# A new order of key tiles in the first attention layer, lent buffers and a second mixer buffer, in a two-layer attention and mixer kernel

## The chip, the cores and the metric

One core of one Trainium2 chip. The metric is the device time of one execution in microseconds (us); medians of several executions are given. Every ratio is to runs of the kernel before on the same chip in the same rounds.

Engines: PE is TensorE, ACT is ScalarE, DVE is VectorE, POOL is GpSimd, SP is the engine whose queue issues most transfers. A "block" below is one 128 x 512 square of attention scores (one head, one tile of 128 keys, 512 queries).

## The reference, cut to what matters

Batch 1, 2048 rows, width 448, 16 heads of 28, bf16 in and out. The same weights serve both layers.

```python
def _A_ref(x, wqkv, wo):                       # attention
    q, k, v = split(x @ wqkv)                  # 16 heads of 28
    p = softmax(q k^T * 28 ** -0.5)            # 2048 x 2048 for each head
    return (p v) @ wo
def _B_ref(x, w1, w2, w3, w4):                 # mixer and MLP
    h = gelu(layernorm(x) @ w1)
    hs = concat(h shifted by -1, +1, -2, +2 rows, a quarter of the columns each) @ w2
    x1 = x + hs
    return x1 + gelu(layernorm(x1) @ w3) @ w4
for layer in range(2):
    x = x + _A_ref(layernorm(x), ...)
    x = x + _B_ref(layernorm(x), ...)
```

## The kernel before

A small scheduler in Python lays out the instructions of all engines before the program is built. Each job (projection of K, evacuation, mixer of a group of tiles, ...) is a generator that yields operations with an assumed duration; the scheduler places them by readiness and priority. The program then gives each engine its list in that order.

The queries are cut into chunks, the keys into tiles of 128. A *segment* is one chunk, one group of four heads and a run of key tiles. `ORDER` lists (chunk, first tile, end tile) in the order in which ScalarE meets them, four head groups each; layer 0 is "layer one":

```python
CHUNKS = {0: [(0, 4), (4, 4), (8, 4), (12, 2), (14, 2)], ...}          # first row tile, row tiles
ORDER = {0: [(0, 0, 4), (0, 4, 8), (0, 8, 16), (1, 0, 16), (2, 0, 16), (3, 0, 16), (4, 0, 16)],
         1: [(0, 0, 7), (1, 0, 7), (0, 7, 11), (1, 7, 11), (0, 11, 16), (1, 11, 16), (2, 0, 16), ...]}
RANK = {...}      # priorities: ('k', layer, c) K and V of a key chunk, ('q', layer, chunk),
                  # ('a', ...) output projection and first half of the mixer, ('b', ...) second half
D_RATE = {...}    # share of blocks whose exponential VectorE takes
```

A segment waits for its Q and for the K of its tiles. A chunk that comes back to later keys needs a correction (`fct`), a shift of its Q, and its partial sum in DRAM:

```python
def seg_ready(si, kts):
    yield ("wait", ("q", L, CHUNKS[L][ch][0] // 4, g))
    if not first:
        yield ("wait", ("qp", si))
    for c in sorted(set(kc_of(L, k) for k in kts)):
        yield ("wait", ("k", L, g, c))
```

ScalarE evaluates blocks in turns of three and two PSUM banks, while VectorE takes a few blocks with an integer trick and a polynomial, five instructions each:

```python
yield op("act", 0.06 + n * w * 0.000833, lambda e, ...: e.activation(out=PT[:, s0:s0 + n, 0:w],
         in_=ps[:, bk[0]:bk[0] + n, 0:w], func=ACT.Exp, scale=SCALE), ...)
```

The mixer's hidden rows of a group of up to four tiles go into one buffer, `h2T`; pairs of tiles of the second layer use idle V slots instead:

```python
side = not direct and L == 1 and n == 2
hname = "h2V" if side else "h2T"
```

PE is kept busy with matmuls on the identity where it has nothing else (`filler`). The scheduler places one when PE's counted load in a short window is under `TARGET`.

## Time and profile before

| | before |
|---|---|
| median | 1077.07 us (1076.42 to 1079.06, 3 runs) |
| profiled span | 1074.8 us |
| ScalarE busy | 1020.3 us (95%) |
| blocks on VectorE | 37 of 2048 |
| ScalarE idle from 17 to 100 us | 9.6 us |
| after the last exponential | 47.5 us |

How to read the profile: a row of a group gives the line, the engine, what it writes and reads, the count, busy time and mean duration, then the idle time of its engine just before it and who ended it. In the views of stretches the engines come in the order PE, PEld (weight loads), DVE, ACT, POOL, then the granted TensorE clock, the DMA share and GB/s. In a timeline the bracket gives the idle time before the first instruction of the row. The lines themselves stand in the prediction.

### The profile page before, as it was taken

The numbers are of one execution on the slowest core, as the hardware profiler recorded it, in microseconds if no ns is written. First come the engines' busy times: TensorE is split into PE (matmuls) and PEld (weight loads), VectorE is DVE, ScalarE is ACT, GpSimd is POOL, SyncE is SP. The second block draws the span as 40 slices with busy tenths as digits, with TensorE's granted clock in tenths as the row PEclk, the third lists the DMA queues.
The fourth block names the chain that finished last, engine by engine and source line by source line (L and its number), as shares of the span: only waits on it lengthen the run. The fifth ranks groups of instructions, "written<-read, shape, count | busy, mean of one in ns | idle before, by whom it ended". The sixth has DMA issues, their size and how long they took to land.

```text
span 1074.8 us, 35355 instructions
## 1 busy us (share of the span) xinstructions
PE 1010.3 (94%) x16037; PEld 422.5 (39%) x16037; DVE 619.8 (58%) x1236; ACT 1020.3 (95%) x920; POOL 312.9 (29%) x506
## 2 busy tenths in 40 slices
PE   7999999999999999999999998999999999999998
PEld 2333443443333433343433433353333433444455
DVE  7776569836468236765156553514797484444442
ACT  6898999999999999999999999999999999999952
POOL 2244125201254024452032201102743130432111
PEclk9999999999999999999999999999999999999999
DMA  4547221103111022120221123313411110220000
GB/s 115 138 110 208 83 57 32 24 17 91 32 32 32 13 78 56 44 42 22 63 58 40 41 85 95 133 50 110 89 27 21 43 39 16 59 49 16 12 11 32
DMA packets 95494, 62.26 MB, mean 58 GB/s; under 512 B 68528, under 2 KB 85248, under 8 KB 95344
## 3 DMA queue, kind: packets, MB, share of 16 engines
q1 hardware_dynamic: 91968, 51.92, 18.7%
q0 software_dynamic: 3376, 8.09, 2.7%
q8 instruction: 125, 2.05, 0.8%
q14 instruction: 25, 0.20, 0.1%
HBM read 27.12 MB, written 15.71 MB: 40 GB/s over the span
## 4 chain that ended last, share of the span: by engine, by line
ACT 72%; PE 18%; DVE 8%; issue 1%; DMA 0%; SPq 0%; DVEq 0%
ACT PT L1455 65%; PE ps L770 11%; ACT h2T L1852 4%; PE ps L1300 4%; PE ps L761 3%; ACT fb L1703 1%; ACT L1852 1%; DVE fb L1364 1%; DVE fb L1362 1%; ACT L1455 1%; DVE hT L1704 1%; DVE fb L1702 1%; DVE yd L1341 1%; DVE PD L1369 1%; DVE xn L962 0%
## 5 line engine op out<-in xcount | busy, mean ns | idle before, releaser
L1455 ACT ACTIVATE PT<-ps 128x1536 bf16<-128x1536 f32 (+1 forms) x805 | 920.8, 1339 | 14.2 <-PE ps L1300 13.2
L1300 PE MATMUL ps<-qT,kT 32*128 32x512 bf16 (+1 forms) x2560 | 315.0, 340 | 28.5 <-ACT PT L1455 19.8
L761 PE MATMUL ps<-PT,vaug 128*32 128x512 bf16 (+1 forms) x2523 | 250.3, 340 | 0.0
L1300 PEld LDWEIGHTS ps<-qT,kT 32*128 32x128 bf16 x2560 | 80.7, 91 | 300.6 <-ACT PT L1455 272.2
L1893 PE MATMUL ps<-ident 128*32 128x256 bf16 x3804 | 166.6, 274 | 3.4 <-POOL ident L850 1.5
L770 PE MATMUL ps<-xT,w 128*32 128x512 bf16 (+2 forms) x1600 | 126.5, 360 | 2.5 <-DVE h2T L1837 1.6
L1893 PEld LDWEIGHTS ps<-ident 128*32 128x32 bf16 x3804 | 107.8, 96 | 31.2 <-issue 12.3
L770 PE MATMUL ps<-w,h2T 128*32 128x448 bf16 x1512 | 106.3, 365 | 13.8 <-ACT h2T L1852 12.9
L1837 DVE CAST h2T<-ps 128x512 bf16<-128x512 f32 (+2 forms) x112 | 67.8, 606 | 79.5 <-PE ps L770 69.8
L761 PEld LDWEIGHTS ps<-PT,vaug 128*32 128x32 bf16 x2523 | 74.8, 95 | 93.4 <-issue 80.4
L1560 POOL TENSOR_TENSOR otn<-ub,fb 128x512 bf16<-128x512 f32 (+1 forms) x36 | 40.2, 1116 | 179.9 <-DMA fb<-rscr 179.7
L1096 POOL TENSOR_TENSOR sq<-kT 128x512 bf16<-128x512 bf16 (+2 forms) x32 | 29.9, 935 | 120.2 <-DVE kT L1110 120.0
L770 PEld LDWEIGHTS ps<-w,h2T 128*32 128x32 bf16 x1512 | 41.1, 98 | 51.7 <-issue 18.4
L1701 POOL TENSOR_TENSOR fb<-hT 112x512 f32<-112x512 bf16 (+1 forms) x36 | 37.5, 1044 | 79.2 <-DVE hT L1684 75.7
L770 PEld LDWEIGHTS ps<-xT,w 128*32 128x32 bf16 x1600 | 43.7, 95 | 42.6 <-issue 18.1
L1341 DVE TENSOR_SCALAR yd<-ps 128x512 int32<-128x512 f32 x37 | 25.1, 682 | 39.5 <-PE ps L1300 39.1
L1787 POOL TENSOR_TENSOR x_res<-x_res,x1b 128x448 f32<-128x448 f32 x32 | 38.9, 1222 | 20.9 <-DVE xn L967 20.8
L1534 DVE COPY ub<-ps 128x512 f32<-128x512 f32 (+1 forms) x40 | 23.3, 582 | 35.1 <-PE ps L761 34.8
L953 POOL TENSOR_SCALAR vpe<-mv 128x1 f32<-128x1 f32 (+2 forms) x21 | 5.5, 261 | 129.2 <-DVE mv L948 129.2
L1852 ACT ACTIVATE h2T<-h2T 128x7168 bf16<-128x7168 bf16 (+2 forms) x8 | 42.0, 5244 | 0.1
L1536 DVE SCALAR_TENSOR_TENSOR ub<-ub,fct,ps 128x512 f32<-128x512 f32 x24 | 17.9, 746 | 41.0 <-PE ps L761 40.7
L770 PE MATMUL ps<-kT,w 128*32 128x512 bf16 (+2 forms) x576 | 40.4, 360 | 1.1 <-DMA kT<-xn 1.0
(168 smaller groups left out, 1208.0 us busy)
## 6 DMA issues: line engine op xcount, KB each, us to landing
uscr<-ub SPq DMA_DIRECT2D x24, 256.0 KB
ub<-uscr SPq DMA_DIRECT2D x24, 256.0 KB
fb<-rscr SPq DMA_DIRECT2D x24, 256.0 KB
xnd<-xn SPq DMA_DIRECT2D x28, 128.0 KB, 2.2
x_res<-in_A_x_dram POOLq DMA_DIRECT2D x16, 224.0 KB, 4.0
xd<-x_res SPq DMA_DIRECT2D x16, 224.0 KB, 2.7
x_res<-xd SPq DMA_DIRECT2D x16, 224.0 KB, 3.0
out_dram<-obf SPq DMA_DIRECT2D x16, 112.0 KB
```

The source lines that it names most:

```text
L761: return lambda e: e.matmul(out=out, lhsT=lhsT, rhs=rhs, start=start, stop=stop, **kw)
L770: r.append(e.matmul(out=out[c:c + w, :], lhsT=lhsT[:, c:c + w], rhs=rhs, start=start, stop=stop, tile_position=(0, c)))
L1096: return op("pool", 0.15 + NW * 0.0018, lambda e: e.tensor_tensor(out=sq[:, si, 0:NW], in0=src, in1=src, op=ALU.mult), reads=rk, writes=[( ...
L1300: yield op("pe", max(0.055, 0.22 / nc_ * NW / 512.0), lambda e, i=i, kc=kc, j=j, g=g, a=a, NW=NW, bank=bank: e.matmul(out=ps[:, bank, i * ...
L1341: yield op("dve", c_ps(512), lambda e: e.tensor_scalar(out=y, in0=ps[:, bi(bank), :], scalar1=SCALE * L2E * FS, scalar2=-126.0 * FS, op0=A ...
L1455: yield op("act", 0.06 + n * w * 0.000833, lambda e, bk=bk, s0=s0, n=n, w=w: e.activation(out=PT[:, s0:s0 + n, 0:w], in_=ps[:, bk[0]:bk[0] ...
L1560: yield op("pool", 0.2 + NW * 0.0021, lambda e: e.tensor_tensor(out=otn[:, g, 0:NW], in0=u, in1=rb[:, 0:NW], op=ALU.mult), reads=[uk, fk], ...
L1701: yield op("pool", 0.2 + NW * 0.00165, lambda e: e.tensor_tensor(out=f, in0=z, in1=z, op=ALU.mult), reads=hk, writes=[fk])
L1787: yield op("pool", 1.2, lambda e: e.tensor_tensor(out=X, in0=X, in1=X1, op=ALU.add), reads=[xk, ("x1b", s)], writes=[xk], deps=[nop_])
L1837: ev = op("dve", c_ps(NW), lambda e, fch=fch, b=b: e.tensor_copy(out=hb[:, fch, 0:NW], in_=ps[:, bi(b), 0:NW]), reads=[("ps", bi(b))], wri ...
L1852: yield op("act", c_act(nl * NW), lambda e: e.activation(out=hb[:, 0:nl, 0:NW], in_=hb[:, 0:nl, 0:NW], func=ACT.Gelu_apprx_tanh), reads=al ...
L1893: return [e.matmul(out=ps[32 * c:32 * c + 32, bi(b), 0:256].rearrange("p (a n) -> p a n", n=128), lhsT=ident[:, 32 * c:32 * c + 32], rhs=i ...
```

## The change

The intent: while K and V of tiles 4 to 15 are still being made, let ScalarE work on the first four key tiles for *two* query chunks, so that the later keys are due later. With it: more buffers for VectorE's exponentials in V slots that are idle for a while, look-ahead of these exponentials over the end of a segment, a second mixer buffer for groups of up to four tiles, and all priorities, rates and margins drawn anew. The loads of w3 and w4 at segment 9 are the same in both kernels. The core of the diff (cut):

```diff
-ORDER = {0: [(0, 0, 4), (0, 4, 8), (0, 8, 16), (1, 0, 16), (2, 0, 16), ...
+ORDER = {0: [(0, 0, 4), (1, 0, 4), (0, 4, 8), (0, 8, 16), (1, 4, 16), (2, 0, 16), ...
-DPRIO = 5
+DPRIO = 1.5
-DSEG = 0
+DSEG = 1
-XSHUT = (10, 50)
+XSHUT = (16, 61)
-RANK = {... [('b', 0, 0), ('a', 0, 0), ('k', 0, 1), ('b', 0, 1), ('k', 0, 2), ('k', 1, 0), ('q', 0, 2), ('q', 0, 1), ...
+RANK = {... [('q', 0, 1), ('b', 0, 1), ('b', 0, 0), ('a', 0, 0), ('k', 1, 0), ('q', 0, 3), ('k', 0, 1), ...
-D_RATE = {(0, 0): 0.08, (0, 1): 0.05, (0, 2): 0.05, (0, 3): 0.06, (1, 0): 0.16, (1, 1): 0.1, (1, 2): 0.16}
+D_RATE = {(0, 0): 0.08, (0, 1): 0.045, (0, 2): 0.05, (0, 3): 0, (1, 0): 0.015, (1, 1): 0.1, (1, 2): 0.03}
-Sched.TARGET = 0.64
+Sched.TARGET = 0.6
-FTH = 0.03
+FTH = 0.15
...                                   # other margins of the scheduler
+        def xtra(kind):
+            for ph, base in ((0, 16), (1, 9)):
+                if ("xopen", ph) in SC.events and ("xshut", ph) not in SC.events:
+                    return {"y": ["yv%d" % base, "yv%d" % (base + 2)], "f": ["fv%d" % (base + 4)], "pd": ["pv%d" % (base + 6)]}[kind]
+            return []
...
-                        got = yield ("try", [MISC[0:2], YS, PDS])
+                        got = yield ("try", [MISC[0:2], xtra("y") + YS, xtra("pd") + PDS])
...
-            side = not direct and L == 1 and n == 2
-            hname = "h2V" if side else "h2T"
...
+                hname = yield ("acq", ["h2T", "h2W"] if ("xdone", 1) in SC.events else ["h2T"], [("xT", xt)])
+                wide = hname == "h2W"
```

A branch that would give blocks to POOL is in the new code as well, but its rates are all 0. Factors and shifts get a pair index (`PI`), because two chunks now come back from different points.

## The prediction

> **What bounds the kernel now.** I read the page first (busy shares, slices, chain), then the waits of ScalarE, then the stretches of the span, then ScalarE's timeline at the start. The page:
>
> ```profile
> span 1074.8 us, 35355 instructions
> PE 1010.3 (94%) x16037; PEld 422.5 (39%) x16037; DVE 619.8 (58%) x1236; ACT 1020.3 (95%) x920; POOL 312.9 (29%) x506
> PE   7999999999999999999999998999999999999998
> ACT  6898999999999999999999999999999999999952
> ACT 72%; PE 18%; DVE 8%; issue 1%; DMA 0%; SPq 0%; DVEq 0%
> ```
>
> ScalarE (ACT) is busy for 1020.3 of 1074.8 us and makes 72% of the chain that ended last. PE shows 94%, but 166.6 us of that are matmuls on the identity that only keep it busy (L1893), so PE has room in most stretches; ACT has none. ACT's work by shape:
>
> ```profile
> L1455 ACT ACTIVATE PT<-ps 128x1536 bf16<-128x1536 f32 x402 | 623.4, 1551 | 6.1 <-PE ps L1300 5.2
> L1455 ACT ACTIVATE PT<-ps 128x1024 bf16<-128x1024 f32 x402 | 453.5, 1128 | 8.1 <-PE ps L1300 8.0
> L1852 ACT ACTIVATE h2T<-h2T 128x7168 bf16<-128x7168 bf16 x4 | 24.7, 6178 | 0.0
> ```
>
> The exponentials come in pairs of three and two blocks of 512. 402 x 3 + 402 x 2 + 1 = 2011 blocks; the problem has 2 layers x 16 heads x 16 key tiles x 4 query chunks = 2048, so 37 blocks go to VectorE (its group for yd has x37, 25 of them between 100 and 340 us, 12 after 500 us). Everything is a question of when ACT is idle. The stretches, engine busy times in the order PE, PEld, DVE, ACT, POOL:
>
> ```profile
> 0.00:17.00 17.00, 10.31 (x111) 4.50 (x111) 11.82 (x50) 10.13 (x14) 6.27 (x19) 1.00 0.65 180
> 17.00:51.00 34.00, 30.23 (x430) 10.84 (x425) 26.89 (x63) 31.56 (x31) 6.43 (x9) 1.00 0.42 103
> 51.00:88.00 37.00, 35.45 (x486) 11.90 (x486) 27.24 (x63) 29.84 (x28) 16.19 (x20) 1.00 0.51 143
> 88.00:180.00 92.00, 87.56 (x1392) 36.19 (x1391) 63.79 (x119) 92.00 (x83) 31.12 (x45) 1.00 0.32 85
> 180.00:520.00 340.00, 320.32 (x5340) 135.12 (x5341) 200.04 (x363) 338.24 (x296) 107.85 (x170) 0.99 0.16 39
> 520.00:780.00 260.00, 250.29 (x3613) 98.34 (x3605) 127.57 (x273) 258.33 (x229) 64.75 (x103) 0.99 0.28 78
> 780.00:1026.00 246.00, 230.23 (x3823) 98.32 (x3820) 144.54 (x274) 243.72 (x211) 70.56 (x120) 1.00 0.14 31
> 1026.00:1074.80 48.80, 45.89 (x860) 27.26 (x860) 17.86 (x38) 16.48 (x34) 9.72 (x21) 1.00 0.07 24
> ```
>
> Length less ACT busy gives its idle time: 6.9 us before the first exponential, 2.4 + 7.2 us from 17 to 88 us, 0.0 + 1.8 + 1.7 + 2.3 us in the 938 us after that, and 32.3 us in the tail after the last exponential. So there are only two places to gain idle time: the first 88 us and the tail. The timeline of ACT between 44 and 96 us shows what the first one is:
>
> ```profile
> 43.55 7.04 ACT L1455 ACTIVATE PT<-ps 128x1024 bf16<-128x1024 f32 x6
> 54.54 11.41 ACT L1455 ACTIVATE PT<-ps 128x1024 bf16<-128x1024 f32 x10 [3.96 <-PE ps L1300]
> 65.92 18.47 ACT L1455 ACTIVATE PT<-ps 128x1024 bf16<-128x1024 f32 x16
> 87.98 7.80 ACT L1455 ACTIVATE PT<-ps 128x1024 bf16<-128x1024 f32 x7 [3.59 <-PE ps L1300]
> ```
>
> Two holes, 3.96 us at 50.6 and 3.59 us at 84.4. They fall where the first query chunk needs keys 4-7, and then keys 8-15: around them PE runs the K and V projections (L770 on wk_pad and wv), and between 60 and 80 us there is not one idle-filling matmul. The score matmuls wait for K, not for ACT.
>
> **What the Trainium skill says.** "ScalarE: Activation LUTs", section "What ACT_TABLE_LOAD costs": an ACTIVATE with immediate operands takes 186 ns + 0.833 ns per element, back-to-back ones overlap by about 93 ns, a table load takes about 1283 ns. The trace agrees roughly: 48 exponentials of 1280 elements on average take 54.45 us from 383.31, so 1.134 us each (1066 ns of elements and 68 ns), and a table load 1283 ns. A block taken from ACT thus saves 0.427 + 0.068/2.5 = 0.454 us.
> "TensorE: Matmul & The Clock Gate", section "What's actually happening": the idle PE is throttled and activity releases it. The granted clock here is 1.00 nearly everywhere, so no gain is to be had there.
> "GPSIMD Engine Reference", section "1. Specifications": its SBUF interfaces are shared with VectorE, so some VectorE instructions meet contention. A normalisation that has a median of 387 ns took 2.22 us at 46.74 while POOL filled wo_pad for 1.59 us from 47.19; that agrees, though one case shows no cause.
>
> **The change part by part.**
>
> *Order of layer one (index 0).* Before: chunk 0 with keys 0-3, then 4-7, then 8-15, then chunk 1 with all. After: chunk 0 with keys 0-3, **chunk 1 with keys 0-3**, then chunk 0 with 4-7 and 8-15, then chunk 1 with 4-15. A step of 4 heads groups x 4 key tiles x 4 heads is 64 blocks = 29 us of ACT at 0.454. So the K and V of tiles 4-7 are due 29 us later, and so are those of 8-15. In their place Q of chunk 1 is due at 50.6 us. Is it there? The transposed load of tiles 4-7 is issued at 35.51 and the first K matmul on it starts at 42.84. Q has the same source. From 42.9: four projection steps 0.9, evacuation 0.74 (L1143), square on POOL 1.04 (L1096), one matmul step 0.4, addition 0.68 (L1172), some 0.2 us of waiting at each of four hand-overs: 4.6 us, so about 47.5. That is 3 us early; its next head groups follow at 7.3 us intervals, which is ample. So the first hole closes. K and V of 4-7, finished at about 60 in the old trace, are then due at 80; those of 8-15, finished at about 88 plus some 6 us for Q put ahead of them (VectorE: 4 x 1.42 = 5.7 us), are due near 109. So the second closes too. 3.96 + 3.59 = 7.55; I keep 1.0 for hitches of the denser PE and VectorE. **-6.5 us**, all on the path.
>
> *What the new order costs.* Four more partial sums of 256 KB are stored to DRAM and fetched (24 -> 28), four more query shifts of 0.35 us on VectorE and one more correction factor on ACT (0.3 us). All but the last lie beside ACT. **+0.3 us.** Chunk 0 ends 29 us later, so its output projection and mixer (some 25 us of PE, estimated from 17-23 us for a mixer group) start later; fillers of 15.8 and 11.3 us in 150-200 and 200-250 leave room.
>
> *Blocks on VectorE.* Each saves 0.454 us of ACT and costs VectorE 0.68 + 0.78 + 0.87 + 0.46 + 0.72 = 3.5 us. Look-ahead across a segment's end (DSEG 1) makes short segments eligible, and idle slots of V serve as two more int32, one more fp32 and two bf16 buffers. Against it the rates fall in layer two (0.16 to 0.015 and to 0.03) and the required share of fillers rises from 0.03 to 0.15. By the rates layer one could take 12 + 16 + 16 = 44 before and took 25; after, 28 + 16 + 16 = 60. Counting a filler of four matmuls as the schedule does, 0.12 us, fillers are 26%, 21%, 17%, 10% in the four stretches of 50 us from 100 (x436, x348, x288, x164), so the threshold bites after 250 us. I estimate 30 in layer one. In layer two only 700-750 (x444, 27%) passes: 11. Total 41, four more: 4 x 0.454 = **-1.8 us.** The pool path is in the code but its rates are all 0: nothing.
>
> *Second wide mixer buffer.* Before, only pairs of tiles of the second layer had another buffer. After, any group may take V slots 9-15 and K slots 9-15, but only once the extra buffers shut at segment 61 (some 920 us), and the third xT buffer is lost then. In the tail 9.0 us of PE are w4 matmuls of the group of tiles 7-10 and 5.8 + 5.8 us those of 11-12. But the group 7-10 did not wait for h2T: the previous group left it at 943.7 us and its own first copy comes at 961.6, then takes until 1008 because PE serves it at low priority. So the buffer gains little: **-1 us**, with 5 us of doubt either way as priorities are drawn anew. The load of w3 and w4 at segment 9 is in the old code as well; 9 now comes about 2 us earlier. Nothing.
>
> Sum: -6.5 + 0.3 - 1.8 - 1.0 = -9.0 us; 1077.07 - 9.0 = **1068 us**.
>
> **The rivals.** *Q takes the place of K.* If Q of chunk 1 comes late (it runs on the VectorE that is 79% busy from 17 to 51 us), the hole at 50.6 stays or grows; for it speaks that two loads of the same tiles now queue; against it the 3 us computed above. Time: 1072 to 1075. *The work comes back in the tail.* PE is 94% busy from 780 to 1026 with few fillers; if ACT is faster but PE is not, mixer work piles up behind the last exponential and the tail grows by what the start won. For it: 20.6 us of mixers already lie there. Against it: PE sees the same gap earlier, and fillers of 21 us from 700 to 750 show slack. Time: 1075. *Everything works*: VectorE takes 60 blocks (-10 us), the mixers of 7-12 leave the tail (-9 us): 1051. *VectorE becomes the bound*: urgent exponentials (priority 1.5 for 5) delay the evacuations and scores stall: 1080 or more.
>
> **Range and chances.** The start term is worth 3 to 8 us, the blocks -5 to +4, tail and mixers -9 to +6. Combined as independent, this gives 1068 with 8 in 10 between 1054 and 1078. Faster by over 2% means below 1055.5 and needs all three to go well: 0.11. Slower by over 2% means above 1098.6: 0.03. Within: 0.86.
>
> **What would show it.** ACT idle from 17 to 100 us at 2 to 4 us for 9.6; no wait over 1 us for score matmuls after 27 us; 35 to 47 yd instructions, the first before 100 us; last exponential near 1018; tail of 45 to 50 us. I am wrong if a hole over 2 us stays at the second step (Q late), if yd counts leave 30 to 52, or if the tail moves by more than 6 us.

## The result, and the profile after

The changed kernel took **1062.9 us** (1062.77 to 1067.52, 4 runs), the kernel before in its four runs 1076.74. The ratio, here as everywhere below, is for the runs of the same rounds, so not quite the ratio of the medians: 0.9881, interval 0.9848 to 0.9913. That is 1.2% faster, within the 2% band, and inside the predicted range.

From the page of the changed kernel (span, busy times, ScalarE in 40 slices, the chain that ended last):

```profile
span 1061.2 us, 34191 instructions
PE 990.3 (93%) x15418; PEld 405.6 (38%) x15421; DVE 628.6 (59%) x1275; ACT 1017.8 (96%) x921; POOL 309.1 (29%) x510
ACT  6999999999999999999999999999999999999962
ACT 75%; PE 16%; DVE 4%; DMA 2%; POOL 1%; issue 1%; SPq 0%; DVEq 0%
```

The second and the fourth digit of the ACT row were 8 and are 9. ScalarE's busy time fell by 2.5 us only (1017.8 for 1020.3), so most of the 13.6 us by which the span shrank are idle time. The two big groups and VectorE's first step for a block:

```profile
L1541 ACT ACTIVATE PT<-ps 128x1536 bf16<-128x1536 f32 x401 | 623.2, 1554 | 6.7 <-PE ps L1311 6.3
L1541 ACT ACTIVATE PT<-ps 128x1024 bf16<-128x1024 f32 x401 | 453.6, 1131 | 0.4 <-PE ps L1311 0.3
```
```profile
L1393 DVE TENSOR_SCALAR yd<-ps x26: 674/692/693, 113.1 to 801.0; 128x512 int32<-128x512 f32 x26
L1393 DVE TENSOR_SCALAR vaug<-ps x16: 667/688/693, 110.7 to 842.5; 128x512 int32<-128x512 f32 x16
```

26 + 16 = 42 blocks are on VectorE, 16 of them through the lent V slots (`vaug`). Now ScalarE's timeline from 35 to 111 us, where the two holes of the kernel before were:

```profile
35.50 42.66 ACT L1541 ACTIVATE PT<-ps 128x1536 bf16<-128x1536 f32 x37
78.06 0.20 ACT L1275 ACTIVATE fct<-dbc 128x4 f32<-128x4 f32 x1
78.15 32.92 ACT L1541 ACTIVATE PT<-ps 128x1024 bf16<-128x1024 f32 x29
```

37 and then 29 exponentials without a bracket: both holes are gone. The same stretches as in the prediction, and the tail of each kernel from the end of its last exponential (first the changed kernel, then the one before):

```profile
17.00:51.00 34.00, 30.74 (x433) 10.76 (x433) 26.85 (x64) 32.08 (x32) 8.56 (x11) 1.00 0.42 102
51.00:88.00 37.00, 36.42 (x471) 11.50 (x468) 25.73 (x57) 36.82 (x34) 15.79 (x19) 1.00 0.47 119
1017.30:1061.20 43.90, 40.68 (x754) 25.54 (x746) 16.66 (x36) 15.00 (x34) 9.66 (x21) 1.00 0.06 21
```
```profile
1027.30:1074.80 47.50, 44.59 (x848) 26.77 (x837) 17.46 (x36) 15.19 (x32) 9.72 (x21) 1.00 0.07 22
```

ScalarE idles 1.9 + 0.2 us instead of 2.4 + 7.2 us in the first two. The tail is 3.6 us shorter, and PE is busy 3.9 us less in it: in both kernels the tail is PE's work plus about 3 us (47.5 - 44.6 and 43.9 - 40.7). Which work? Groups of PE in these two tails, before and after:

```profile
L770 PE MATMUL ps<-w,h2T 128*32 128x448 bf16 x160 | 8.5, 353 | 0.0
L770 PE MATMUL ps<-w,vaug 128*32 128x448 bf16 x112 | 5.8, 353 | 0.0
L761 PE MATMUL ps<-xT,w 128*128 128x256 bf16 x42 | 5.4, 273 | 0.0
```
```profile
L762 PE MATMUL ps<-xT,w 128*128 128x256 bf16 x52 | 6.5, 273 | 0.0
L771 PE MATMUL ps<-w,h2T 128*32 128x448 bf16 x112 | 5.8, 354 | 0.0
L771 PE MATMUL ps<-w,kT 128*32 128x448 bf16 x28 | 1.9, 354 | 0.0
L771 PE MATMUL ps<-w,vaug 128*32 128x448 bf16 x28 | 1.7, 354 | 0.0
```

One tile needs 56 of these w4 matmuls. Before, nearly three tiles of the group 7-10 (in `h2T`, 160) and both of 11-12 (in `vaug`, 112) were left when the last exponential ended. After, the group 7-10 sits in the wide buffer (`kT` and `vaug`), and only one tile of it (28 + 28) is left. That is 4.9 us less, and 1.1 us more of w3 (52 for 42).

The ledger of the spans, -13.6 us in all: the last exponential ends at 1017.3 for 1027.3 (-9.9), the tail is 43.9 for 47.5 (-3.7 from unrounded times). The -9.9 are idle time from 17 to 100 us, 2.1 for 9.6 (-7.5), and five more blocks on VectorE at 0.454 us (-2.3, worked out, not measured). Idle time between 100 us and the last exponential is 5.5 for 5.7.

### The profile page after: what moved, and what is told of

Same layout as the page of the kernel before. It is cut to its first block, busy times and chain, and to the rows that moved or that the text cites. A ratio compares the mean times of both kernels' runs of the same rounds, so it can differ in the third digit from the quotient of the medians.

```text
span 1061.2 us, 34191 instructions
## 1 busy us (share of the span) xinstructions
PE 990.3 (93%) x15418; PEld 405.6 (38%) x15421; DVE 628.6 (59%) x1275; ACT 1017.8 (96%) x921; POOL 309.1 (29%) x510
## 3 DMA queue, kind: packets, MB, share of 16 engines
q8 instruction: 121, 1.98, 0.8%
## 4 chain that ended last, share of the span: by engine, by line
ACT 75%; PE 16%; DVE 4%; DMA 2%; POOL 1%; issue 1%; SPq 0%; DVEq 0%
ACT PT L1541 68%; PE ps L771 9%; PE ps L1311 4%; ACT h2T L1955 3%; PE ps L762 3%; ACT fb L1789 1%; ACT L1955 1%; ACT L1541 1%; DMA xT<-xnd 1%; DVE st L949 1%; DMA rT<-ub 0%; DMA PT<-in_A_wqkv_dram 0%; DMA xT<-xn 0%; PE ps L1996 0%; ACT vaug L1955 0%
## 5 line engine op out<-in xcount | busy, mean ns | idle before, releaser
L771 PE MATMUL ps<-xT,w 128*32 128x512 bf16 (+2 forms) x1952 | 148.3, 357 | 2.9 <-DMA xT<-xn 1.1
L1996 PE MATMUL ps<-ident 128*32 128x256 bf16 x3188 | 144.8, 274 | 2.3 <-POOL ident L851 1.5
L1933 DVE CAST h2T<-ps 128x384 bf16<-128x384 f32 (+2 forms) x98 | 58.3, 595 | 87.7 <-PE ps L771 77.9
L1996 PEld LDWEIGHTS ps<-ident 128*32 128x32 bf16 x3188 | 89.5, 96 | 28.9 <-issue 12.7
L771 PEld LDWEIGHTS ps<-xT,w 128*32 128x32 bf16 (+1 forms) x1952 | 53.0, 95 | 47.9 <-issue 23.7
L1098 POOL TENSOR_TENSOR sq<-qT 128x512 bf16<-128x512 bf16 x28 | 29.6, 1060 | 58.7 <-DVE qT L1145 54.2
L771 PE MATMUL ps<-xT,wk_pad 128*32 128x512 bf16 (+1 forms) x512 | 42.5, 376 | 0.5 <-DVE kmaxc L1123 0.4
L1700 DVE TENSOR_TENSOR x_res<-x_res,ps 128x448 f32<-128x448 f32 x32 | 19.8, 619 | 38.9 <-PE ps L771 38.6
L771 PE MATMUL ps<-xT,wq_pad 128*32 128x512 bf16 x448 | 41.4, 392 | 0.8 <-DMA xT<-xnd 0.6
L771 PE MATMUL ps<-wo_pad,otn 128*32 128x448 bf16 x512 | 38.9, 361 | 2.5 <-DVE x_res L1700 2.0
```

The source lines that it names most:

```text
L771: r.append(e.matmul(out=out[c:c + w, :], lhsT=lhsT[:, c:c + w], rhs=rhs, start=start, stop=stop, tile_position=(0, c)))
L1098: return op("pool", 0.15 + NW * 0.0018, lambda e: e.tensor_tensor(out=sq[:, si, 0:NW], in0=src, in1=src, op=ALU.mult), reads=rk, writes=[( ...
L1933: ev = op("dve", c_ps(NW), lambda e, hr=hr, vw=vw, b=b: e.tensor_copy(out=hr, in_=vw(ps[:, bi(b), 0:NW])), reads=[("ps", bi(b))], writes=h ...
L1996: return [e.matmul(out=ps[32 * c:32 * c + 32, bi(b), 0:256].rearrange("p (a n) -> p a n", n=128), lhsT=ident[:, 32 * c:32 * c + 32], rhs=i ...
```

## The experiments

All twelve runs gave correct results. One thing was not foreseen: *any* edit of order or priorities makes the scheduler lay out the whole program anew, so each run differs from its neighbour in more than its edit. The table therefore reads each trace in parts; in its column of the tail the busy time of PE is in brackets. "Clock lost" is the sum of (1 - granted clock) x length over stretches of 4 us from 100 us on. The expectations below call this number "us at half clock"; that was loosely put: the time actually spent at half clock is twice the number.

| run | median us | ratio to before | last exp ends | ACT idle 17-100 | ACT idle 100 to last exp | tail (PE busy in it) | blocks on DVE | clock lost |
|---|---|---|---|---|---|---|---|---|
| before | 1074.8 to 1076.8 | 1 | 1027.3 | 9.6 | 5.7 | 47.5 (44.6) | 37 | 3.4 |
| changed | 1062.90 | 0.9881 | 1017.3 | 2.1 | 5.5 | 43.9 (40.6) | 42 | 3.4 |
| order_alone | 1103.46 | 1.0263 | 1044.3 | 22.0 | 17.2 | 57.0 (52.8) | 35 | 6.8 |
| order_q_first | 1085.60 | 1.0079 | 1030.7 | 4.3 | 21.1 | 56.9 (52.8) | 35 | 15.4 |
| order_q_margin | 1075.79 | 1.0012 | 1020.9 | 3.9 | 14.0 | 53.2 (50.1) | 35 | 6.8 |
| order_ranks | 1070.45 | 0.9961 | 1011.1 | 3.8 | 6.5 | 56.1 (52.2) | 42 | 0.0 |
| old_order | 1094.57 | 1.0159 | 1038.1 | 10.3 | 23.5 | 56.9 (52.5) | 38 | 14.0 |
| no_wide | 1068.11 | 0.9932 | 1018.9 | 2.4 | 7.0 | 47.1 (43.3) | 42 | 3.4 |
| no_dve_exp | 1087.47 | 1.0131 | 1031.1 | 2.1 | 9.8 | 54.4 (50.7) | 0 | 3.4 |
| no_extra_buffers | 1084.03 | 1.0081 | 1031.7 | 2.1 | 21.6 | 48.7 (44.9) | 47 | 2.1 |
| drawn_1 | 1074.37 | 0.9979 | 1023.8 | 2.1 | 13.8 | 43.9 (40.6) | 48 | 8.5 |
| drawn_2 | 1063.26 | 0.9878 | 1018.2 | 2.1 | 8.8 | 43.8 (40.6) | 47 | 5.1 |
| drawn_3 | 1069.62 | 0.9934 | 1024.9 | 2.2 | 13.8 | 43.8 (40.6) | 48 | 6.8 |
| drawn_landing | 1067.84 | 0.9921 | 1021.2 | 3.6 | 17.3 | 43.8 (40.6) | 68 | 13.6 |

The columns from "last exp ends" on come from one profiled execution each. Its spans lie 0.4 to 6.7 us from the medians, so single microseconds of the table are not to be compared across rows with the medians. The clock lost differs between executions of *one* program too: the four of drawn_1 have a mean granted clock of 0.992, 0.989, 0.981 and 0.978 (8.5 to 23.7 us lost, worked out as (1 - clock) x span) and spans of 1067.7, 1069.3, 1076.0 and 1077.4 us. Their instructions are the same, so no layout is behind this difference. The column "clock lost" is therefore one draw for each version, and for drawn_1 the lowest of four. My theory before the runs: the gain of the start is the order's, because K and V are due later. The rival: the order only swaps one deadline for another, and the new priorities, buffers and rates make the gain.

### The order alone

```diff
 # the kernel before
-ORDER = {0: [(0, 0, 4), (0, 4, 8), (0, 8, 16), (1, 0, 16), ...
+ORDER = {0: [(0, 0, 4), (1, 0, 4), (0, 4, 8), (0, 8, 16), (1, 4, 16), ...
 # and the pair index PI for factors and shifts
```

> The kernel before with the new order of layer one alone (and the pair index it needs); priorities, rates and buffers stay. Theory A (the holes are deadlines of K and V, and the order alone moves them): both holes close, ScalarE is idle for 2 to 3 us from 17 to 100 us instead of 9.6, 7 us faster, 1070. Theory B (the order only swaps the deadline of K for one of Q, and the priorities, which still put Q of chunk one behind two K projections, decide whether Q is there): with two xT buffers taken by the K loads of tiles 4-7 and 8-11, Q is loaded after about 60 us, a hole of 10 to 17 us opens at 50.6, and the time is 1080 to 1090.

Measured: 1103.46 us, 2.6% slower. ScalarE's timeline (the hole is the bracket of the second row):

```profile
46.46 3.88 ACT L1462 ACTIVATE PT<-ps 128x1536 bf16<-128x1536 f32 x3
64.47 0.20 ACT L1271 ACTIVATE fct<-dbc 128x4 f32<-128x4 f32 x1 [14.13 <-DVE dbc L1280]
65.75 7.80 ACT L1462 ACTIVATE PT<-ps 128x1024 bf16<-128x1024 f32 x7 [1.08 <-PE ps L1307]
```

One hole from 50.3 to 65.7 us, 14.1 + 1.1 us of idle time, right where chunk 1's first scores are due. The first correction of Q of chunk 1 on VectorE (L1172) starts at 64.60 and ends 0.68 us later; the scores follow. Theory A falls: the order alone makes the start worse, 22.0 us of idle time for 9.6. Theory B is right on the hole's size (the time, 1103, is over its 1080 to 1090), but wrong on the way: I expected the *load* of Q's rows to wait for a buffer; in the trace two transposed loads are issued at 35.26, one behind the other, and the next at 56.84. The rows were there. What was late were Q's projections and evacuations, which stood behind those of K by priority: the first evacuation of this Q (L1143) starts at 58.22, after K's (L1110) at 50.88, 54.88 and 57.56. In addition the factor `fct`, which needs K of tiles 4-7, stood ahead of the exponentials in ScalarE's list and shows as what ended the wait.

### The order, with Q of chunk one first

```diff
 # order_alone
-RANK = ... [('b', 0, 0), ('a', 0, 0), ('k', 0, 1), ..., ('q', 0, 2), ('q', 0, 1), ('k', 1, 2), ...
+RANK = ... [('q', 0, 1), ('b', 0, 0), ('a', 0, 0), ('k', 0, 1), ..., ('q', 0, 2), ('k', 1, 2), ...
```

> The same, with Q of chunk one moved to the front of the priorities and nothing else. Theory B: the hole at 50.6 is gone or under 2 us, the one at 84.4 as well, ScalarE idle from 17 to 100 us is 2 to 4 us; 37 blocks on VectorE as before, within 5; so 6 to 8 us faster than before, 1069, if the tail stays within 3 us of 47.5. Theory A expects the same time as of the order alone. If it is the other parts of the change (buffers, rates) that made the gain, it stays at 1075 or more.

Measured: 1085.60 us. Half of the expectation holds: idle time from 17 to 100 us is 4.3 us, one hole of 1.78 us is left. One entry in a list of priorities was worth 17.7 us of idle time. But the kernel is 0.8% *slower* than before, 17 us over the expected 1069. Part of the time is lost later (idle time from 100 us to the last exponential is 21.1 us for 5.7), and the tail is 9.4 us longer, with a gelu over `h2T` of 5.32 us in it (at 1052.28), where in the kernel before the gelu over `h2T` ran ahead of the last exponential (at 1011.49). A timeline of PE and the stretches around the first spell (engines and clock in the order given above):

```profile
242.84 0.61 PE L761 MATMUL ps<-PT,vaug 128*32 128x512 bf16 x5
246.17 1.15 PE L770 MATMUL ps<-xT,w 128*32 128x384 bf16 x12 [2.72 <-issue]
```
```profile
243.50:246.20 2.70, 0.03 (x4) 0.06 (x8) 2.27 (x3) 1.22 (x2) 1.87 (x2) 0.79 0.03 4
246.20:248.00 1.80, 1.80 (x19) 0.52 (x23) 0.00 (x0) 0.10 (x1) 0.00 (x0) 0.50 0.49 127
248.00:250.00 2.00, 2.00 (x21) 0.55 (x17) 0.56 (x1) 1.73 (x2) 0.00 (x0) 0.50 0.00 0
```

PE stands for 2.72 us at a w3 matmul that reads a transposed tile (xT); the view names no releaser ("issue"). The next score matmuls for ScalarE stand behind it in PE's list. ScalarE idles for 1.5 us in the first stretch and 1.7 us in the second, until these scores are made; that is still the standstill. The granted clock is 0.50 from 245 to about 252 us, and with PE busy throughout ScalarE idles for another 1.6 us from 248 to 252. There are five such spells between 100 us and the last exponential in this run (from 245, 764, 883, 989 and 1023 us; the last lies in the stretch 1024 to 1028 with a clock of 0.66), two short ones in the kernel before. From here on there was a new theory (C): late transfers block PE, the clock falls, ScalarE starves. The trace bears it out in part only. The spells at 245, 764 and 883 follow a standstill of 1.9 to 2.7 us at a matmul on xT. Those at 989 and 1023, which make 6.8 of the 15.4 us lost, do not; the longest pause of PE in the 5 us before the one at 989 is this:

```profile
987.18 0.39 PE L1307 MATMUL ps<-qT,kT 32*128 32x256 bf16 x4 [0.52 <-ACT PT L1462]
989.43 0.61 PE L1307 MATMUL ps<-qT,kT 32*128 32x256 bf16 x4
```

### The same, with more time allowed for transposed loads

```diff
 # order_q_first; assumed durations of the scheduler, not the work
-TR_T = 2.6
-TRL_T = 5.4
-Sched.DOUBT = {"dma": 0.8, ...
+TR_T = 3.4
+TRL_T = 6.4
+Sched.DOUBT = {"dma": 1.6, ...
```

> The version with the new order and Q first, with more time allowed for transposed loads when the instructions are laid out (3.4 for 2.6, 6.4 for 5.4 us, and a margin of 1.6 for 0.8 us); same work. That version was slower than before although its two holes were closed. Theory C (the gain was lost because PE stood blocked 2 to 3 us on late transposed loads, its clock then fell to half for some 3.4 us, and ScalarE starved: 15.4 us at half clock after 100 us for 3.4 in the kernel before): with later placed matmuls the time at half clock falls to 3 to 8 us, and the kernel reaches 1068 to 1074. Theory D (the new order without the other parts costs more elsewhere, for example by the later mixers of chunk zero): the half clock may fall, the time stays at 1080 or more.

Measured: 1075.79 us, 9.8 us better than order_q_first, level with the kernel before. Clock lost fell from 15.4 to 6.8 us, idle time in the middle from 21.1 to 14.0. That is the direction and about the size of Theory C. None of the three spells left follows a matmul on xT: PE had stood for 4.04 us at a correction of Q before the one at 304 us, and behind a gelu before those at 386 and 536. But the two spells that were not Theory C's are gone as well, so the new layout, and not the margins alone, may have moved them. It did not come to the 1068 to 1074 hoped for: the margins themselves give idle time at full clock (3.1 and 1.8 us in two stretches at 688 and 692 us), and the tail is still 53.2 us. D is not refuted for this rest.

### The order with all of the new priorities

```diff
 # order_alone
-RANK, Q_LEAD of the kernel before
+RANK, Q_LEAD of the changed kernel
```

> The kernel before with the new order and all of the new priorities and lead times of Q, without new buffers, rates and margins. If priorities are what the order needs, 1065 to 1072 with at most 5 us at half clock after 100 us; if half-clock spells come back in any layout that was not tuned on the chip, 1078 to 1090 with 10 us or more of them. ScalarE idle from 17 to 100 us is 2 to 4.5 us in both.

Measured: 1070.45 us, 0.4% faster than before. This run separates the parts best. It has no lent buffers, no new rates, no wide mixer buffer, yet no clock was lost in the profiled execution (the fastest of three; the others have a mean clock of 0.998 and 0.997), idle time to 100 us is 3.8, and 42 blocks are on VectorE, as many as in the changed kernel. Its last exponential ends at 1011.1 us, *earlier* than the changed kernel's 1017.3. And its tail is 56.1 us for 43.9. Part of the two is one thing: a group's gelu over 6656 elements (5.74 us, at 1012.92) and its table load come after the last exponential here and before it in the changed kernel. So end of exponentials and tail are no independent terms; only their sum counts. The new order with the new priorities gives about a third of the gain (ratio 0.9961 against 0.9881).

### The old order in the changed kernel

```diff
 # the changed kernel
-ORDER = {0: [(0, 0, 4), (1, 0, 4), (0, 4, 8), (0, 8, 16), (1, 4, 16), ...
+ORDER = {0: [(0, 0, 4), (0, 4, 8), (0, 8, 16), (1, 0, 16), ...
```

> The changed kernel with the old order of layer one. If the order brings the 7.5 us, both holes are back (ScalarE idle 9 to 10 us from 17 to 100 us) and the time is 1070, half of the gain gone. If the gain came from priorities, rates and buffers, it stays within 3 us of 1063.

Measured: 1094.57 us. Idle time from 17 to 100 us is back at 10.3 us, as expected. The time is 24 us over the expected 1070: 14.0 us of clock lost (five spells between 100 us and the last exponential), 23.5 us idle in the middle, and a tail of 56.9. The verdict on record is unclear (ratio 1.0115 to 1.0202 around the 2% line, clearly slower than before). order_alone and old_order together suggest that the priorities of the change are not good as such but fit the new order. How much of the 24 us is chance of the layout no run tells.

### One mixer buffer

```diff
 # the changed kernel
-                hname = yield ("acq", ["h2T", "h2W"] if ("xdone", 1) in SC.events else ["h2T"], [("xT", xt)])
+                hname = yield ("acq", ["h2T"], [("xT", xt)])
```

> The changed kernel with one mixer buffer, h2T alone. My prediction gave the second buffer 1 us. If the shorter tail (43.9 us for 47.5) comes from it, because the w4 matmuls of tiles 7-10 leave the tail, the tail grows by 3 to 5 us and the time is 1066 to 1068; if from the priorities drawn anew, it stays within 1 us of 1063. The last exponential should end within 1 us of 1017 in both.

Measured: 1068.11 us (ratio 0.9932 against 0.9881 for the changed kernel, with other runs of before, so some 5 us). The tail is 47.1 us for 43.9, with 2.7 us more of PE work in it, as the first reading expects. The rest is earlier: idle time in the middle is 1.5 us more, with a spell at 752 us that the changed kernel did not have. The last exponential ends 1.6 us later, where within 1 us was expected. The layout is close to that of the changed kernel up to there, so in this pair of traces the wide buffer goes with 3 us of tail; of the other 2 us the trace shows the place, not that the buffer caused it. The intervals of the two ratios overlap (0.9894 to 0.9971, 0.9848 to 0.9913), so the whole 5 us are not clear of noise.

### No exponentials on VectorE

```diff
 # the changed kernel
-D_RATE = {(0, 0): 0.08, (0, 1): 0.045, ...}
+D_RATE = {}
```

> The changed kernel with no exponentials on VectorE: 42 blocks return to ScalarE at 0.454 us, so 19 us if each is on the path: 1082. Much less (under 1072) would mean that the blocks on VectorE do not set the time; more than 1088 would mean half-clock spells on top.

Measured: 1087.47 us, over the expected 1082 and 24.6 us more than the changed kernel (spans: 1085.5 - 1061.2 = 24.3). The 42 blocks account for 19.1 us at 0.454 us each. Idle time in the middle is 4.3 us more. The two sum to 23.4 us; the last exponential is only 13.8 us later and the tail 10.5 us longer, because a whole group's gelu falls after that line here (3.18 and 2.75 us, from 1032.86) and before it in the changed kernel. In this run PE had 50.7 us of work left instead of 40.6. The price of a block holds within the noise of the layout; a clean measure of it this run is not.

### No lent buffers

```diff
 # the changed kernel, in xtra()
-                if ("xopen", ph) in SC.events and ("xshut", ph) not in SC.events:
+                if False:
```

> The changed kernel with the idle V slots no longer lent to the exponentials on VectorE. If these buffers are what lets VectorE take blocks, the count of first steps falls from 42 to 30 or fewer and the time grows by 5 us or more; if the rates and the look-ahead decide it, the count stays within 5 of 42 and the time moves only by what the layout does to half-clock spells.

Measured: 1084.03 us, but the count of blocks *rose* to 47. So the buffers are not what lets VectorE take blocks. Of the 19.2 us by which the span grew, 13.2 were lost at one place of ScalarE's timeline:

```profile
547.59 11.41 ACT L1541 ACTIVATE PT<-ps 128x1536 bf16<-128x1536 f32 x10
572.16 8.23 ACT L1541 ACTIVATE PT<-ps 128x1536 bf16<-128x1536 f32 x7 [13.16 <-PE ps L1311]
```

A hole of 13.2 us in layer two, ended by score matmuls at 571.72 just behind the correction of a Q (L1174) at 570.97. It is the hole of order_alone again, at another chunk: the layout put that Q behind mixer work. For what the buffers are worth in an equal layout the run is inconclusive.

### Three more draws of the priorities

```diff
 # the changed kernel; new RANK, Q_LEAD, D_RATE, FTH, TARGET, XSHUT, GSL, AGED (some of them in each)
```

These were layouts that the scheduler's own assumed durations ranked ahead of the changed kernel's.

> The changed kernel with another draw of priorities, rates of VectorE and target share of PE; order, buffers and work are the same. It is to beat both kernels. More blocks on VectorE (47 or so for 42, 2.3 us less on ScalarE) and a tail of 43 to 46 us would give 1058 to 1061 if at most 4 us at half clock come after 100 us. If the ranking of layouts does not survive late transposed loads (Theory C), 8 us or more at half clock and 1066 to 1080.

> Another draw, nearer to the changed kernel (a dozen places in the priorities differ). As for the draw before: 1059 to 1062 without half-clock spells beyond 4 us, 1066 to 1080 with them.

> A third draw, farther from the changed kernel, with the lent V slots closing at segments 14 and 62. As for the two before: 1059 to 1062 without half-clock spells beyond 4 us, 1066 to 1080 with them.

Measured: 1074.37, **1063.26** and 1069.62 us. All three have 47 or 48 blocks on VectorE, 2.1 or 2.2 us idle in the start and a tail of 43.8 or 43.9. They differ by the middle: 13.8, 8.8, 13.8 us of idle time with 8.5, 5.1, 6.8 us of clock lost. drawn_2 ties with the changed kernel (0.9878 and 0.9881 to before) and falls between the two ranges expected; it wins five blocks (2.3 us) and has 3.3 us more idle time in the middle. The queue of SP and PE's timeline at that spell:

```profile
190.03 0.60 SPq L1637 DMA_DIRECT2D rscr<-rT  x1
193.57 0.55 SPq L1642 DMA_DIRECT2D fb<-rscr  x1
194.16 1.19 SPq L974 DMA_TRANSPOSE xT<-xn  x1
```
```profile
195.86 0.51 PE L1996 MATMUL ps<-ident 128*32 128x256 bf16 x12
199.28 1.04 PE L771 MATMUL ps<-xT,w 128*32 128x512 bf16 x8 [2.90 <-issue]
```

SP issues in order. The read of `rscr` waits until its write has landed, 3.5 us after its issue at 190.03; the layout assumed 1.9 us. The transposed load behind it goes out at 194.16, although its rows were normalised by 192.5. Then PE waits 2.9 us for it, and the clock is 0.50 in the stretch from 200 to 204 us. ScalarE was idle for 5.1 us from 196 to 208. Here the links stand in one trace: a small transfer that lands late, a transfer behind it in the same queue, a matmul at the head of PE's list, the clock, ScalarE. The first link accounts for at most 1.6 of the 2.9 us (194.16 less 192.54); PE starts only 5.1 us after the load's issue, where these loads land after 2.8 us in the median of this trace, so the load was slow as well, for a reason not shown. Nor is the first link the rule: of the 36 writes of `rscr` in this trace, the dependent read follows the issue by 1.77 us in the median (1.98 us in the changed kernel), and by 3 us or more in seven.

### A draw with measured landing times

```diff
 # the changed kernel
-  ... writes=[("rT",)], t=1.9, iss=0.57)
+  ... writes=[("rT",)], t=2.9, iss=0.57)
-  ... writes=[("rscr", rk)], t=1.9)
+  ... writes=[("rscr", rk)], t=3.3)
 # new RANK, Q_LEAD, D_RATE, XSHUT (14, 56), DPRIO 5, FTH 0.03, GSL 0.2, TARGET 0.64
```

> The changed kernel laid out anew with the small transfers of the normalisation (sums to DRAM) counted as landing after 2.9 and 3.3 us, as the traces have them (3.1 and 3.5), instead of 1.9, and with priorities, rates and closing points drawn again under that; the same work, 68 blocks on VectorE instead of 42. If too short times for transfers were what put PE behind late loads (Theory C), half-clock spells after 100 us stay under 6 us, 26 more blocks save up to 12 us on ScalarE, and the kernel beats both: 1048 to 1058. If spells are a matter of luck in every new layout, 8 us or more of them and 1062 to 1075, as in the draws before.

Measured: 1067.84 us. A miss: 68 blocks did go to VectorE and ScalarE is busy for 1008.4 us instead of 1017.8, but 13.6 us of clock were lost and the middle idles for 17.3 us. What ScalarE no longer had to do, it spent waiting. The second corrected duration was a misreading: 3.5 us are what the slow writes take, while the 1.9 us of before fit the usual one (see drawn_2). So the run is no fair test of Theory C. What it does show is the last branch of its expectation: spells in a new layout again. VectorE is also busier (67% for 59%), and no run tells its share apart. No version beat the changed kernel.

## Why the prediction was right or wrong, point by point

- **What bounds it** (ScalarE, with idle time in the start and the tail only): right. The gain of 13.6 us in the span is 7.5 us of start, about 2.3 us of blocks and 3.7 us of tail; the middle did not move.
- **The order** (-6.5 us): right in mechanism, 1.0 us too small. Both holes closed, -7.5 us; no hitch of the 1.0 us that I had kept back appeared. Working out that Q would be there at 47.5 us was near: the first correction of Q (L1174) ended at 49.2 us. The margin before 50.6 was not the 3 us that I gave it, but 1.4. What the prediction did not say is that it holds only because Q of chunk 1 leads the new priorities: order_alone shows the first rival ("Q takes the place of K") at full size, 15 us.
- **The cost of the order** (+0.3 us): 28 partial sums and five factors are in the trace. No run shows their cost alone.
- **Blocks on VectorE** (-1.8 us by 41 blocks): 42, so -2.3 us. That the count was right is luck: 25 of them are in layer one, where 30 were predicted, and 17 in layer two, where 11 were; the errors cancelled. (In the kernel before the two counts are 24 and 13, not 25 and 12.) Nor is the reason shown: order_ranks reached 42 with the old rates, without look-ahead and lent buffers, and no_extra_buffers 47.
- **The second mixer buffer** (-1 us, 5 us of doubt): this term was mis-sized. It failed by its size: the tail shrank by 3.7 us, and without the buffer (no_wide) it is 3.2 us longer. I had argued that group 7-10 did not wait for `h2T` in the kernel before. That reading holds (943.7 and 961.6 us), but it did not bound the gain: in the changed kernel the gelu of this group starts 19.5 us before the last exponential ends, for 15.8 before, and one tile of its w4 work is left after it, for nearly three. What of this is the buffer and what the priorities is not shown. The doubt covered it. One label of the prediction is wrong, not its sum: of the "5.8 + 5.8 us" of tiles 11-12 one is w4 (112 matmuls), the other w3.
- **w3 and w4** ("9 comes about 2 us earlier"): the loads went out at 85.2 us instead of 99.3, 14 us earlier. It had no visible effect.
- **The rivals.** "The work comes back in the tail": not in the changed kernel, but in every version that puts the new order into the kernel before (tails of 53 to 57 us). "VectorE becomes the bound": no sign. The largest risk was not among my rivals: spells at half clock. I had written that the clock is 1.00 nearly everywhere, "so no gain is to be had there". As a gain that was right; as a loss it counts: between the four executions of drawn_1, one program, 15.2 us more of clock lost go with 9.7 us more of span. In seven of the eight other versions with four executions or more the slowest execution has the lowest clock too (not in drawn_3).
- **The sum**: -9.0 predicted, -13.9 measured in the medians (1076.74 - 1062.90); in the range, and 5 us off in the centre by the start (1 us), the blocks (0.5) and the tail (2.7), the rest being rounding and the median of before.

What stays open: what starts a spell, and how much of the difference between the layouts is chance of the execution, since only one execution of each was traced. The chain is in the trace at one spell of drawn_2, and at the first spell of order_q_first only PE's part of it. Spells also follow a standstill behind a gelu (2.13 and 2.29 us, below), which no run took away, or no standstill at all (989 us in order_q_first).

## What to carry to other kernels

When an engine that must never wait has holes early on, look for which input is due there and give it work that needs an input already made; then make sure that the new work's own input leads the priorities, since otherwise the hole only moves and grows. In a program laid out in advance, judge an edit by its parts in the trace (start, middle, tail, clock), because each edit moves all the others. And where a queue runs in order, one short transfer that lands late can hold up the transfer behind it, and then the matmul. Before a layout is judged by its half-clock spells, look at more than one execution of it.

## What the Trainium skill lacked or had wrong

- "TensorE: Matmul & The Clock Gate", section "What's actually happening", gives the cold state after at least one idle window of about 3.4 us. Here shorter gaps were enough: 2.13 us (before, at 374.2), 2.29 us (changed kernel, at 889.4), 2.72 us (order_q_first) and 2.90 us (drawn_2) were each followed by a granted clock of about 0.5. The length of the pause alone does not decide: 2.29 us at 358.7 in the changed kernel and 2.50 us at 377.7 in no_dve_exp were followed by a clock of 1.00, and the spell at 989 in order_q_first came after no pause over 0.52 us. The length of a spell agrees: the spell in the kernel before lasts some 3.4 us (0.73, 0.50 and 0.91 in three stretches of 2 us from 376 us), that of order_q_first about twice this.
- No section of that page says what such a spell does to another engine: with PE busy for all of it, ScalarE idled for 1.6 of the 4.0 us from 248 to 252 us in order_q_first, although it needs only the scores (0.61 us for a turn of them, 0.39 at full clock).
- "DMA: Bandwidth & Descriptors", section "Anatomy of one DMA — SWDGE (gpsimd) path", puts the fixed cost of a DMA at about 2.0 us for that path. The writes of `rscr` here (4 or 8 KB, issued by SP) come near it in the median: in drawn_2 the dependent read is issued 1.77 us after them. What the page lacks is the spread of a whole transfer: 1.71 to 4.73 us in that trace, 3.54 at the spell shown, which is too wide to lay out a queue by one figure.
- "ScalarE: Activation LUTs", section "What ACT_TABLE_LOAD costs": the table load of 1283 ns was right to the nanosecond; its further 1380 ns of drain do not show here: in the changed kernel the gelu at 997.86 starts 1.30 us after the load at 996.56, and the load 0.02 us after the exponential before it.
